# Chunk attention, Fourier mix and MLP on one core: a rest tile mixed in one piece, four transform parts open at once, last stores on two queues

## The chip, the cores and the metric

The kernel runs on 1 core of one Trainium2 chip. Its time is the device time of one execution in microseconds (us), as the median of several runs. A profile is a record of one execution on the same hardware; its span runs from the first to the last instruction of the core.

## The reference

The inputs are `q`, `k`, `v` of shape (8, 8, 576, 64), that is 8 sequences, 8 heads, 576 tokens and 64 features a head, and two MLP weights. Attention is within chunks of 64 tokens; the heads are then put side by side, so that `x` has 8 sequences of 576 tokens with 512 features, and this follows:

```python
X = np.fft.fft(x, axis=1)          # over the 576 tokens
X = np.fft.fft(X, axis=2)          # over the 512 features
mixed = np.real(X).astype(np.float32)
u = x + mixed
mu = np.mean(u, axis=-1, keepdims=True)
var = np.mean((u - mu) ** 2, axis=-1, keepdims=True)
un = (u - mu) / np.sqrt(var + 1e-06)
ch = np.maximum(un @ w_ch1, 0.0) @ w_ch2     # 512 -> 2048 -> 512
return (u + ch).astype(np.float32)
```

All of it is in float32.

## The kernel before, in words

**Tiles and groups.** The tokens lie in tiles of 128 rows. A sequence has 9 chunks of 64 tokens: two LO tiles (chunks from the front), two HI tiles (chunks from the back, held mirrored), and its middle chunk, which shares a "rest" tile (kind `RE`) with the middle chunk of the next sequence. There are 8 groups of four tiles, one for each sequence, and a ninth group, the last, of the four rest tiles. The MLP runs over the groups in turn: `up_first`, `up_plain` and `down_plain` for the first ones, `up_halves` and `down_halves` for the others, where each matrix product is done as seven products of half matrices (lines 1017 and 1064) and weights are fetched from DRAM again for each group.

**Who does what in between.** While the MLP of one group keeps TensorE busy, the attention and the Fourier mix of the next sequence `b` are made in a side generator (`side`, attention and then `fourier(b)`). The loop at the end of the kernel takes one step of the MLP, then so many steps of the side generator as are due. The order of instructions on each engine is this written order; no scheduler changes it. So a step of `fourier` on TensorE stands between two steps of the MLP, and what ScalarE must copy for it has the length of an MLP step to be done.

**The Fourier mix.** Symmetry folds the tokens and features first (`fold`): for each sequence there are two tiles `pm` with 128 token rows, and `pm_rest` for the middle chunk, with 64 token rows for each of its entries. `pm_rest` holds parts 0 and 2 on rows 0 to 63 and parts 1 and 3 on rows 64 to 127. Then:

- The token transform makes four parts T = 0 to 3 (even and odd features, cosine and sine). `product` (line 647) multiplies the fold with the table `tk`: for each part two products over 128 rows with 289 columns, and one over 64 rows with 289 columns. The 64-row products use one half of the array's rows, and those of even and of odd T use different halves. For part 2 there are 12 more, each with a single output row of about 73 columns (`mids`), on four column parts of the array; they write into free columns of part 2's PSUM bank.
- Each part is held in one PSUM bank. The kernel before opens two banks (`z`, from the pool `ps_t` of two), makes parts 0 and 1, lets ScalarE copy them out, takes one step of the MLP, and then makes parts 2 and 3 with `mids` in the same two banks.
- ScalarE copies each part into `zf` (256 columns, line 672) and `zr` (33 and 31 columns, lines 673 and 675: the middle chunk's tokens). `zr` has a half `h` for each of the two sequences that share a rest tile.
- The feature transform `mixed(i)` (line 699) multiplies the columns of `zf`, 128 at a time, with the four tables `ce`, `co`, `cx`, `so`. This gives one 128 by 512 tile in PSUM. For an odd sequence it starts with the rest tile (`i == NM`), made before in two halves of 64 rows with four products each.
- `y`, `both` and `added` add the result to `x`, `means` takes the statistics, and `normed` and `turned` make the MLP's input of it.

The first sequence has a function of its own, `fourier_early`, which opens all four parts at once already (lines 744 and 747), before the MLP starts.

**The end.** The last group's tiles are rest tiles. `store` writes each as two chunks, and each chunk as 63 rows and one row, all issued by SyncE (lines 864 and 865). The last tiles are ready when the last of TensorE's products has been added by VectorE (line 1084).

Of the kernel before, what the change touches and what calls it, by code (L numbers as in the profile page):

```python
# [8 lines left out]
FP32 = mybir.dt.float32  # L9
U32 = mybir.dt.uint32  # L10
ACTF = mybir.ActivationFunctionType
# [5 lines left out]
def kernel(  # L17
# [32 lines left out]
    nc = tc.nc  # L50
    B, H, S, D = q.shape
    DM = H * D
    DFF = w_ch1.shape[1]
    CH = 64
    NC = S // CH
    NM = 2
# [5 lines left out]
    HM, HQ = DM // 2, DM // 4  # L62
    NQ = S // 2 + 1
    NS = (NQ + 3) // 4
    NL = 128 * NM
# [3 lines left out]
    scale = 1.0 / float(D) ** 0.5  # L69

    const = ctx.enter_context(tc.tile_pool(name="const", bufs=1))
# [4 lines left out]
    ps_t = ctx.enter_context(tc.tile_pool(name="ps_t", bufs=2, space=bass.MemoryType.PSUM))  # L76
    ps_a = ctx.enter_context(tc.tile_pool(name="ps_a", bufs=1, space=bass.MemoryType.PSUM))
# [8 lines left out]
    ce = const.tile([128, HQ + 1], FP32, name="ce")  # L86
    co = const.tile([128, HQ], FP32, name="co")
    cx = const.tile([128, HM], FP32, name="cx")
    so = const.tile([128, HQ], FP32, name="so")
# [36 lines left out]
    groups = [[at[what, b, i] for i in range(NM) for what in (LO, HI)] for b in range(B)]  # L126
# [35 lines left out]
    start = one_p.tile([128, KF * 512], FP32, tag="big", name="start")  # L162
# [459 lines left out]
        yield ready(hi)  # L622


    zr = const.tile([128, 2, 4, CH], FP32, name="zr")

    def means(ns):
        st = sm_p.tile([128, 2, 2], FP32, tag="st", bufs=6 + NP, name="st")
# [10 lines left out]
    def fourier(b):  # L639
        h = b % 2  # L640
        zf = one_p.tile([128, 4 * NL + 64], FP32, tag="zf", name="zf")
        zf = zf[:, 0:4 * NL].rearrange("p (t f) -> p t f", t=4)
        pm = [pms.pop((b, i)) for i in range(NM + 1)]

        def product(T, i, out_, lhsT, start, stop, cols=slice(0, NQ)):
            p = slice(0, 128) if i < NM else slice(T % 2 * CH, T % 2 * CH + CH)
            nc.tensor.matmul(
                out=out_, lhsT=lhsT[p], rhs=tk[p, i, T // 2 if T != 5 else 0, cols],
                start=start, stop=stop, skip_group_check=True,
            )  # L650

        for pair in range(2):
            z = [ps_t.tile([128, 512], FP32, tag="pt", name="z") for _ in range(2)]
            for k in range(2):
                T = 2 * pair + k
                for i in range(NM):
                    product(T, i, z[k][:, 0:NQ], pm[i][:, T * HQ:(T + 1) * HQ], i == 0, False)
            for k in range(2):
                product(2 * pair + k, NM, z[k][:, 0:NQ], pm[NM][:, pair * HQ:(pair + 1) * HQ], False, True)
            mids = []  # L660
            if pair == 1:

                for g, c0 in enumerate(range(0, NQ, NS)):
                    c1 = min(c0 + NS, NQ)
                    mids.append((c0, c1, z[0][32 * g:32 * g + 1, NQ:NQ + c1 - c0]))
                for i in range(NM + 1):
                    for c0, c1, out_ in mids:
                        one = pm[i][:, DM:DM + 1] if i < NM else pm[i][:, 2 * HQ:2 * HQ + 1]
                        product(5, i, out_, one, i == 0, i == NM, slice(c0, c1))
            for k in range(2):  # L670
                T = 2 * pair + k
                nc.scalar.copy(zf[:, T, :], z[k][:, 0:NL])
                nc.scalar.copy(zr[:, h, T, 0:NQ - NL], z[k][:, NL:NQ])
                upper, mirrored = zr[:, h, T, NQ - NL:CH], z[k][:, NQ - 2:NL:-1]
                nc.scalar.activation(out=upper, in_=mirrored, func=ACTF.Copy, scale=-1.0 if pair else 1.0)
                for c0, c1, from_ in mids if k == 0 else ():
                    n = max(0, min(c1, NL) - c0)
                    if n > 0:
                        nc.scalar.copy(zf[0:1, T, c0:c0 + n], from_[:, 0:n])
                    if c1 > NL:  # L680
                        nc.scalar.copy(zr[0:1, h, T, 0:NQ - NL], from_[:, n:])
                        nc.scalar.copy(zr[0:1, h, T, NQ - NL:CH], from_[:, NQ - 2 - c0:NL - c0:-1])
            yield

        def mixed(i):
            mix = ps_t.tile([128, 512], FP32, tag="pt", name="mix")
            if i == NM:
                parts = [(j * CH, CH, zr[:, j]) for j in range(2)]
            else:
                parts = [(0, 128, zf[:, :, 128 * i:128 * (i + 1)])]  # L690
            for p0, np_, zt in parts:
                o = mix[p0:p0 + np_]
                for T, (cols, tab) in enumerate((
                    (slice(0, HM + 1, 2), ce),
                    (slice(1, HM, 2), co),
                    (slice(0, DM, 2), cx),
                    (slice(HM + 1, DM, 2), so),
                )):
                    nc.tensor.matmul(
                        out=o[:, cols], lhsT=zt[:, T], rhs=tab,  # L700
                        start=(T == 0), stop=(T == 3), skip_group_check=True,
                    )
            y = three_p.tile([128, XW], FP32, tag="y", name="y")
            nc.scalar.copy(y[:, 0:HM + 1], mix[:, 0:HM + 1])
            nc.scalar.copy(y[:, DM:DM + 1], mix[:, 0:1])
            return y, mix

        def both(y, mix):
            nc.vector.tensor_tensor(out=y[:, DM - 1:HM:-1], in0=y[:, 1:HM], in1=mix[:, HM + 1:DM], op=ALU.subtract)
            nc.vector.tensor_tensor(out=y[:, 1:HM], in0=y[:, 1:HM], in1=mix[:, HM + 1:DM], op=ALU.add)  # L710
            return y

        def added(y, n):
            x, w = xt(n), DM + (kind(n) == HI)
            eng = nc.gpsimd if kind(n) == HI else nc.vector
            eng.tensor_tensor(out=x[:, 0:w], in0=y[:, 0:w], in1=x[:, 0:w], op=ALU.add)  # L716

        for i in ((NM,) if h == 1 else ()) + tuple(range(NM)):
            y = both(*mixed(i))
            ns = [rests[b // 2]] if i == NM else [at[LO, b, i], at[HI, b, i]]  # L720
            for n in ns:
                added(y, n)
            means(ns)
            yield

    def fourier_early():
# [3 lines left out]
        zf = one_p.tile([128, 4 * NL + 64], FP32, tag="zf", name="zf")  # L730
        zf = zf[:, 0:4 * NL].rearrange("p (t f) -> p t f", t=4)
        pm = [pms.pop((0, i)) for i in range(NM + 1)]
        z = [ps_t.tile([128, 512], FP32, tag="pt", name="z") for _ in range(2)]
        more = ps_a.tile([128, 2, 512], FP32, tag="att", name="more_z")
        z += [more[:, k] for k in range(2)]
        mid = ps_f.tile([128, 512], FP32, tag="ff", name="mid")
        mids = [(c0, min(c0 + NS, NQ)) for c0 in range(0, NQ, NS)]
        order = (1, 0, NM)
        for i in order:
            at_ = {"start": i == order[0], "stop": i == order[-1], "skip_group_check": True}  # L740
            for T in range(4):
                p = slice(0, 128) if i < NM else slice(T % 2 * CH, T % 2 * CH + CH)
                d0_ = T * HQ if i < NM else T // 2 * HQ
                nc.tensor.matmul(out=z[T][:, 0:NQ], lhsT=pm[i][p, d0_:d0_ + HQ], rhs=tk[p, i, T // 2], **at_)
            p, d0_ = (slice(0, 128), DM) if i < NM else (slice(CH, 128), 2 * HQ)
            for r, (c0, c1) in enumerate(mids):
                nc.tensor.matmul(
                    out=mid[32 * r:32 * r + 1, 0:c1 - c0], lhsT=pm[i][p, d0_:d0_ + 1], rhs=tk[p, i, 0, c0:c1], **at_
# [8 lines left out]
        for r, (c0, c1) in enumerate(mids):  # L757
            n, from_ = min(c1, NL) - c0, mid[32 * r:32 * r + 1]
# [2 lines left out]
            else:  # L761
                nc.scalar.copy(zf[0:1, 2, c0:c0 + n], from_[:, 0:n])
        for T in range(4):
            nc.scalar.copy(zr[:, 0, T, 0:NQ - NL], z[T][:, NL:NQ])
            upper, mirrored = zr[:, 0, T, NQ - NL:CH], z[T][:, NQ - 2:NL:-1]
            nc.scalar.activation(out=upper, in_=mirrored, func=ACTF.Copy, scale=1.0 if T < 2 else -1.0)
            if T == 2:
                n = NL - c0
                nc.scalar.copy(zr[0:1, 0, T, 0:NQ - NL], from_[:, n:c1 - c0])
                nc.scalar.copy(zr[0:1, 0, T, NQ - NL:CH], from_[:, NQ - 2 - c0:n:-1])  # L770
        yield
        for i in range(NM):
            for T, tab in ((0, cos_d), (1, cos_d), (3, sin_d), (2, sin_d)):
                nc.tensor.matmul(
                    out=early_xp[0][i][:, T % 2::2], lhsT=zf[:, T, 128 * i:128 * (i + 1)], rhs=tab[:, T % 2::2],
# [78 lines left out]
    def store(n, o):  # L854

        if kind(n) == LO:
            b, c = chunks(n)[0]
            to = out[b, c * CH + 1:c * CH + 129, :].rearrange("(c p) d -> c p d", c=2)
            nc.sync.dma_start(out=to[:, ::-1], in_=o)
            return  # L860
        for h, (b, c) in enumerate(chunks(n)):
            r0, t0 = h * CH, c * CH
            if kind(n) == RE:
                nc.sync.dma_start(out=out[b, t0 + 1:t0 + CH, :], in_=o[r0 + 1:r0 + CH])
                nc.sync.dma_start(out=out[b, 0:1, :], in_=o[r0:r0 + 1])
            else:
                nc.sync.dma_start(out=out[b, t0:t0 + CH, :], in_=o[r0:r0 + CH])

# [248 lines left out]
    with tc.manual_schedule():  # L1117
# [73 lines left out]
        t = 0  # L1191
# [84 lines left out]
```

## Time and profile before

| what | value |
|---|---|
| time, median of 3 runs | 1115.54 us (1113.27 to 1116.66) |
| span of the profiled execution | 1113.4 us |
| TensorE products (PE) busy | 1085.2 us, 97% |
| VectorE (DVE) busy | 582.7 us, 52% |
| ScalarE (ACT) busy | 297.7 us, 27% |
| GpSimd (POOL) busy | 277.7 us, 25% |
| granted clock of TensorE | 1.0 |
| `z` products of line 647, 128 rows x 289 columns | 112 records, mean 407 ns |
| rest's `mix` products of line 699, 64 columns of the array | 64 records |

A float32 product leaves two records in the trace, so counts there are twice those in the program. The duration of a record is its latency; records overlap, and what a product costs TensorE is read from the distance between starts. In lines of the timeline the columns are the start and the length in us, the engine, the line of the kernel, the operation, output and inputs, shapes, the number of records, and in brackets idle time before it with what ended it. "SPq" is SyncE's queue of DMA issues.

### The profile page before, as it was taken

What the parts mean: (1) busy time and instruction counts of PE and PEld (TensorE: products, weight loads), DVE (VectorE), ACT (ScalarE), POOL (GpSimd) and SP (SyncE); (2) the same over time, 40 slices, a digit from 0 to 9 for tenths busy, and PEclk for the clock granted to TensorE, in tenths of its full rate; (3) what the DMA queues carried; (4) which work ended last, traced back from release to release, by engine and by line L of the source; (5) the groups of instructions that cost most, each with busy time, mean ns of one, the idle gap of its engine ahead of it and who ended that gap; (6) DMA issues with size and microseconds to landing.
All of it is one profiled execution on the core that took longest, in us unless ns stands there. A gap on an engine that the chain in (4) does not pass through costs nothing. (4 is left out here: it accounts for less than half of the span.)

```text
span 1113.4 us, 18823 instructions
## 1 busy us (share of the span) xinstructions
PE 1085.2 (97%) x7042; PEld 848.6 (76%) x7042; DVE 582.7 (52%) x1260; ACT 297.7 (27%) x725; POOL 277.7 (25%) x403
## 2 busy tenths in 40 slices
PE   8899999999999999999999999999999999999998
PEld 6644454447887888888888888788888888888887
DVE  4799987324556365653555355625554434323521
ACT  4688553222112311322022212221133102201210
POOL 4200102454305140244024220424042401120130
PEclk9999999999999999999999999999999999999999
DMA  8766556689567546682558356763653355446232
GB/s 164 229 184 193 159 157 225 186 244 296 175 176 201 155 138 197 200 244 107 171 167 236 121 170 206 195 188 130 198 171 109 114 167 189 137 152 198 86 114 76
DMA packets 147970, 192.73 MB, mean 173 GB/s; under 512 B 66126, under 2 KB 104014, under 8 KB 140712
## 3 DMA queue, kind: packets, MB, share of 16 engines
q1 hardware_dynamic: 145768, 190.46, 56.3%
q8 instruction: 56, 0.92, 0.3%
q0 software_dynamic: 512, 0.68, 0.3%
q10 hardware_dynamic: 1600, 0.39, 0.2%
q14 instruction: 34, 0.28, 0.1%
HBM read 167.22 MB, written 24.12 MB: 172 GB/s over the span
## 5 line engine op out<-in xcount | busy, mean ns | idle before, releaser
L923 POOL TENSOR_TENSOR h<-h 128x256 f32<-128x256 f32 x64 | 55.8, 878 | 272.6 <-PE pb L1017 153.1
L1064 PE MATMUL pa<-wb,h 128*128 128x256 f32 x512 | 114.8, 381 | 0.0
L1064 PE MATMUL pb<-wb,h 128*128 128x256 f32 x512 | 114.2, 380 | 0.0
L1017 PE MATMUL pb<-unT,wa 128*128 128x256 f32 x448 | 107.0, 382 | 4.1 <-DVE wa L1026 3.7
L1017 PE MATMUL pb<-wa 128*128 128x256 f32 x448 | 107.5, 383 | 2.5 <-DVE h L1034 2.5
L1064 PEld LDWEIGHTS pa<-wb,h 128*128 128x128 f32 x512 | 96.2, 190 | 14.2 <-issue 1.6
L1017 PE MATMUL pa<-unT,wa 128*128 128x256 f32 x448 | 106.6, 381 | 0.0
L1064 PEld LDWEIGHTS pb<-wb,h 128*128 128x128 f32 x512 | 96.1, 190 | 12.5
L1017 PEld LDWEIGHTS pb<-unT,wa 128*128 128x128 f32 x448 | 84.1, 190 | 19.3 <-DVE wa L1026 8.3
L1017 PEld LDWEIGHTS pb<-wa 128*128 128x128 f32 x448 | 83.6, 190 | 16.1 <-DVE h L1034 3.7
L1017 PEld LDWEIGHTS pa<-unT,wa 128*128 128x128 f32 x448 | 84.0, 190 | 11.1
L933 PE MATMUL up<-unT,wa 128*128 128x512 f32 x128 | 58.0, 600 | 2.0 <-ACT h L941 1.2
L971 PE MATMUL dn<-wb,h 128*128 128x512 f32 x128 | 57.6, 598 | 1.3 <-ACT h L941 1.3
L1064 PE MATMUL pa<-wb,yall 128*128 128x256 f32 x256 | 58.2, 382 | 0.0
L1064 PE MATMUL pb<-wb,yall 128*128 128x256 f32 x256 | 57.1, 381 | 0.0
L950 PE MATMUL up<-unT,wa 128*128 128x512 f32 x128 | 56.8, 596 | 0.0
L1064 PE MATMUL pb<-wb 128*128 128x256 f32 x256 | 56.6, 379 | 0.0
L1032 ACT ACTIVATE h<-pa 128x256 f32<-128x256 f32 x56 | 21.5, 383 | 131.3 <-PE pa L1017 131.3
L1024 DVE TENSOR_TENSOR wa<-pa,wa 128x256 f32<-128x256 f32 x56 | 23.8, 425 | 61.4 <-PE pa L1017 60.0
L1017 PE MATMUL pa<-wa 128*128 128x256 f32 x224 | 53.2, 381 | 0.7 <-ACT wa L1022 0.7
L1064 PEld LDWEIGHTS pb<-wb,yall 128*128 128x128 f32 x256 | 48.2, 190 | 6.5
L1064 PEld LDWEIGHTS pb<-wb 128*128 128x128 f32 x256 | 48.3, 190 | 6.2
(235 smaller groups left out, 1664.9 us busy)
## 6 DMA issues: line engine op xcount, KB each, us to landing
wb<-s SPq DMA_DIRECT2D x56, 1024.0 KB
wa<-s SPq DMA_DIRECT2D x196, 256.0 KB
xall<-in_moe_w_ch_dram SPq DMA_DIRECT2D x22, 512.0 KB
q<-in_q_dram SPq DMA_DIRECT2D x96, 112.0 KB
k<-in_k_dram SPq DMA_DIRECT2D x96, 112.0 KB
v<-in_v_dram SPq DMA_DIRECT2D x124, 64.0 KB
yall<-in_moe_w_ch_dram SPq DMA_DIRECT2D x10, 512.0 KB
s<-wb SPq DMA_DIRECT2D x20, 256.0 KB
```

What stands on the lines that cost most here:

```text
L923: nc.gpsimd.tensor_tensor(out=h1[:, m, hi], in0=h1[:, m, lo], in1=h1[:, m, hi], op=ALU.subtract)
L933: nc.tensor.matmul(out=up, lhsT=w1[:, kk, m * 128:(m + 1) * 128], rhs=unT[:, kk], start=(kk == 0), stop=(kk == KD - 1),)
L950: nc.tensor.matmul(out=up, lhsT=w1[:, kk, m * 128:(m + 1) * 128], rhs=unT[:, kk], start=(kk == 0), stop=(kk == KD - 1),)
L971: nc.tensor.matmul(out=dn, lhsT=h1[:, m, s * 128:(s + 1) * 128], rhs=w2[:, m, :], start=(m == 0), stop=(m == KF - 1),)
L1017: nc.tensor.matmul(out=dst, lhsT=w[:, kk, r], rhs=rhs[o][:, kk], start=(o in (0, 2) and kk == 0), stop=(kk == 1), skip_group_check=True,)
L1024: nc.vector.tensor_tensor(out=b, in0=dst, in1=a, op=ALU.add)
L1032: nc.scalar.activation(out=h1[:, m, lo], in_=dst, func=ACTF.Relu)
L1064: nc.tensor.matmul(out=dst, lhsT=lhs[:, m], rhs=w[:, m], start=(o in (0, 2) and m == 0), stop=(m == HF - 1), skip_group_check=True,)
```

## The change

There are three parts. First, `zr` is laid out with the two sequences' halves side by side in each part, so the rest tile is mixed as 128 rows in four products, where there were eight with 64 rows. Second, all four parts of the token transform are open at once: parts 2 and 3 get the two PSUM banks of the attention's scores (`ps_a`, tag "att"). The first step makes the 128-row products of parts 0 and 1, the second step those of parts 2 and 3, then the 64-row products of all four parts one after the other, then `mids`, and then ScalarE copies all four parts out. So all products on parts of the array stand together. Third, for the second and the fourth tile of the last group, the second chunk's stores are issued by ScalarE and not by SyncE.

```diff
-    zr = const.tile([128, 2, 4, CH], FP32, name="zr")
+    zr = const.tile([128, 4, 2, CH], FP32, name="zr")
...
-        for pair in range(2):
-            z = [ps_t.tile([128, 512], FP32, tag="pt", name="z") for _ in range(2)]
-            for k in range(2):
-                T = 2 * pair + k
-                for i in range(NM):
-                    product(T, i, z[k][:, 0:NQ], pm[i][:, T * HQ:(T + 1) * HQ], i == 0, False)
-            for k in range(2):
-                product(2 * pair + k, NM, z[k][:, 0:NQ], pm[NM][:, pair * HQ:(pair + 1) * HQ], False, True)
...
+        z = [ps_t.tile([128, 512], FP32, tag="pt", name="z") for _ in range(2)]
+        more = ps_a.tile([128, 2, 512], FP32, tag="att", name="more_z")
+        z += [more[:, k] for k in range(2)]
+        for T in range(4):
+            for i in range(NM):
+                product(T, i, z[T][:, 0:NQ], pm[i][:, T * HQ:(T + 1) * HQ], i == 0, False)
+            if T == 1:
+                yield
+        for T in range(4):
+            product(T, NM, z[T][:, 0:NQ], pm[NM][:, T // 2 * HQ:(T // 2 + 1) * HQ], False, True)
...
+        for T in range(4):
+            nc.scalar.copy(zf[:, T, :], z[T][:, 0:NL])
+            nc.scalar.copy(zr[:, T, h, 0:NQ - NL], z[T][:, NL:NQ])
...
-            if i == NM:
-                parts = [(j * CH, CH, zr[:, j]) for j in range(2)]
-            else:
-                parts = [(0, 128, zf[:, :, 128 * i:128 * (i + 1)])]
-            for p0, np_, zt in parts:
-                o = mix[p0:p0 + np_]
...
+            zt = zr.rearrange("p t h f -> p t (h f)") if i == NM else zf[:, :, 128 * i:128 * (i + 1)]
+            for T, (cols, tab) in enumerate((
...
             if kind(n) == RE:
-                nc.sync.dma_start(out=out[b, t0 + 1:t0 + CH, :], in_=o[r0 + 1:r0 + CH])
-                nc.sync.dma_start(out=out[b, 0:1, :], in_=o[r0:r0 + 1])
+                eng = nc.scalar if n in groups[-1][1::2] and h else nc.sync
+                eng.dma_start(out=out[b, t0 + 1:t0 + CH, :], in_=o[r0 + 1:r0 + CH])
+                eng.dma_start(out=out[b, 0:1, :], in_=o[r0:r0 + 1])
```

`fourier_early` changes only in the indices of `zr`.

## The prediction

> **What bounds the kernel now.** I read the totals first, then the chain that ended last, then TensorE's timeline around one token transform, the rest tile's mix, ScalarE's timeline beside them, the waits, and the last microseconds.
>
> ```profile
> PE 1085.2 (97%) x7042; PEld 848.6 (76%) x7042; DVE 582.7 (52%) x1260; ACT 297.7 (27%) x725; POOL 277.7 (25%) x403
> ...
> 1094.92 13.83 PE pb L1064 x64
> ...
> 1108.84 0.42 DVE wb L1084
> ...
> 260.39 2.11 PE L647 MATMUL z<-tk,pm 128*128 128x289 f32 x8
> 262.43 0.76 PE L647 MATMUL z<-tk,pm_rest 64*128 64x289 f32 x4
> 263.12 3.72 PE L1064 MATMUL pa<-wb,h 128*128 128x256 f32 x16
> 266.68 2.11 PE L647 MATMUL z<-tk,pm 128*128 128x289 f32 x8
> 268.72 0.76 PE L647 MATMUL z<-tk,pm_rest 64*128 64x289 f32 x4
> 269.40 0.43 PE L647 MATMUL z<-tk,pm 128*1 128x73 f32 x16
> ...
> 270.00 3.72 PE L1064 MATMUL pa<-wb,yall 128*128 128x256 f32 x16
> 273.56 0.39 PE L699 MATMUL mix<-ce,zf 128*128 128x129 f32 x2
> ```
>
> TensorE is busy for 97% of the span, no other engine for more than 52%, and the chain from 884 us to the end is TensorE alone, followed by one addition and the last stores. So time taken from TensorE's order comes off the end, one for one. The waits view supports it: TensorE waits some 23 us in all, in pieces of at most 2.4 us, and none of the waits after the first 20 us is for a DMA.
>
> The eight lines are sequence 2's transform. A stretch costs what lies between its start and the next one's: first step 260.39 to 263.12, 2.73 us, second step 266.68 to 270.00, 3.32 us.
>
> ```profile
> 36.82 1.14 PE L744 MATMUL z<-tk,pm 128*128 128x289 f32 x4
> 37.79 1.14 PE L744 MATMUL more_z<-tk,pm 128*128 128x289 f32 x4
> ...
> 39.10 0.76 PE L744 MATMUL z<-tk,pm_rest 64*128 64x289 f32 x4
> 39.69 0.66 PE L744 MATMUL more_z<-tk,pm_rest 64*128 64x289 f32 x4
> 40.27 0.31 PE L747 MATMUL mid<-tk,pm_rest 64*1 64x73 f32 x8
> ```
>
> This is the first sequence's transform, which has its four 64-row products in a row already: 39.10 to 40.27, 1.17 us for 8 records. Two such products, 4 records, cost 0.68 us above (262.43 to 263.12, 268.72 to 269.40). Four 128-row records in full mode take 37.79 - 36.82 = 0.97 us, so eight take 1.94.
>
> ```profile
> 388.08 0.43 PE L699 MATMUL mix<-ce,zr 128*64 128x129 f32 x2
> ...
> 389.81 3.72 PE L1064 MATMUL pa<-wb,yall 128*128 128x256 f32 x16
> 393.37 0.39 PE L699 MATMUL mix<-ce,zf 128*128 128x129 f32 x2
> ...
> 394.47 0.81 PE L1064 MATMUL pa<-wb,yall 128*128 128x256 f32 x3
> ```
>
> The rest tile's mix in two halves holds TensorE for 1.73 us, the mix of a full tile with the same four tables for 1.10 us.
>
> ```profile
> 151.54 2.22 PE L647 MATMUL z<-tk,pm 128*128 128x289 f32 x8 [0.81 <-ACT zr L675]
> ...
> 271.94 0.22 ACT L675 ACTIVATE zr<-z 128x31 f32<-128x31 f32 x1
> ...
> 1109.29 0.28 SPq L864 DMA_DIRECT2D out_dram<-wb  x1
> ...
> 1110.23 0.28 SPq L865 DMA_DIRECT2D out_dram<-wb  x1
> ```
>
> The first line is the one transform where TensorE waits for ScalarE to free the two banks (sequence 1). The second is the last of ScalarE's copies after sequence 2's second step: it ends at 272.16, and the mix that needs it starts at 273.56. The last two are SyncE's first and last issue of the four stores that follow the last addition.
>
> **What the Trainium skill says.** "TensorEngine Tiling (Array Packing)", Tiling Modes, says that a change of tiling mode drains TensorE. The trace agrees, and gives the price. Entry: four `more_z` records are followed after 1.07 us and not 0.97 (37.79 to 38.86), 0.09 to 0.10. Return: 16 MLP records after a mix of 64 columns take 393.37 - 389.81 = 3.56 us, and in full mode 3.46 (274.65 to 278.11), 0.10. "TensorE: Matmul & The Clock Gate", Part 3, says that products on different row groups run at once, and that weights load beside a running product only when the row group differs or a background buffer is free. The trace agrees for the halves by rows: two products take 0.68 us, which is two passes of 0.24 and a load and a drain of 0.10 each. For the halves by columns it agrees only in part: 1.73 us is far over half of what the same products would take one after the other. "DMA: Bandwidth & Descriptors", Issuing engines are not separate DMA queues, says that a second issuing engine saves only the time to issue. Here that is 0.3 us a store.
>
> **The change part by part.**
>
> First step of the transform. It loses the 64-row products of parts 0 and 1, with both changes of mode. Before: 2.73 us and 0.10 for the return in the MLP step behind it, 2.83. After: eight full-mode records, 1.94. It saves 0.89.
>
> Second step. It gets those two products, in the stretch that is on half the array anyway. By the first sequence's lines four of them take 1.17 us, so 1.17 - 0.68 = 0.49 more. The 12 `mids`, the drain and the return stay. The net of both steps is 0.89 - 0.49 = 0.40 us. Seven sequences use this code (1 to 7): **2.8 us**. All of it is TensorE's own time between MLP steps, so it is on the path. If parts 2 and 3 did not run behind parts 0 and 1 without a new drain, they would cost 0.68, the net would be 0.21, and seven make 1.5. I take 0.40, since the very order was measured.
>
> Rest's mix. Before: the entry of 0.09, then 1.73, then the return of 0.10, that is 1.92 us. After: as a full tile, 1.10, with no change of mode. It saves 0.82 us. Sequences 1, 3, 5 and 7 do it: **3.3 us**. The new layout of `zr` puts the 128 weights of a part side by side as in `zf`; ScalarE's copies keep their count and shapes.
>
> The wait of sequence 1. The step before it starts at 147.03 and its 8 records take 3.53 us elsewhere (160.33 to 163.86), so the second step was due at 150.56 and starts at 151.54; that step is then 3.43 us and not 3.32. With banks of its own, part 2 need not wait for ScalarE: 0.98 + 0.11 = 1.09 us at most. But ScalarE is still in the last weight conversions then (152.55 to 154.54), and all copies are now behind them. TensorE would reach the rest's mix at about 157.0 (144.30 + 1.94 + 3.43 + 3.81 + 3.53); copies that start at 154.5 and take 2.9 us end at 157.4. The four products of the mix wait for their parts one by one, so that 0 to 0.5 us comes back. I take **0.9 us**.
>
> ScalarE's burst. Copies of all four parts now stand in one step. In order of its queue: parts 0 and 1 take 0.87 us (263.22 to 264.1), parts 2 and 3 with the small rows 2.0 (270.14 to 272.16). ScalarE takes instructions strictly in order, so what stands behind the burst is the MLP's copy `wa<-pa`, the copy `y` and the statistics, and the mix waits for the burst. For even sequences one MLP step of 3.56 us lies in between. Parts 0 and 1 don't wait for `mids`: in the first sequence the first copy starts at 39.88, 0.78 us after the 64-row products began. So they are done while TensorE runs the rest of the step, and the end of the burst stays where it is, 1.4 us ahead of the mix. Even if they began only at the step's end, 2.9 us would fit in 3.56. For odd sequences after the first, 6.9 us lie in between. Cost: 0.
>
> Banks. `more_z` takes the bank pair of the scores. The attention of the same sequence has ended by then, and the next one's scores start after the last mix, at least two MLP steps of 3.5 us behind the copies. `z` stays open over one MLP step, in which nothing is turned (the MLP's input of the next group is turned after the mix). Cost: 0.
>
> Last stores. SyncE issues four stores in a row, at 1109.29, 1109.61, 1109.91 and 1110.23; data move from 1110.0 to 1112.0 and the span ends at 1113.4. With two of them on ScalarE, idle by then, the last issue starts at about 1109.61, 0.62 us earlier. The same DMA engines carry both chunks, so the data may take longer once they overlap: 0 to 0.6, and I take **0.5 us**. The other tile's stores are 3 us before the end and cost nothing.
>
> The sum is 2.8 + 3.3 + 0.9 + 0.5 = 7.5 us, and 1115.5 - 7.5 = 1108.0 us.
>
> **The rivals.**
>
> *The halves don't run on.* Parts 2 and 3 pay a load and a drain of their own (1.5 and not 2.8), and overlapping stores bring nothing: 1.5 + 3.3 + 0.9 = 5.7, 1109.8 us. Against it: the first sequence's lines.
>
> *ScalarE's burst becomes the wait.* The copies begin late, behind relu or conversions, and the mix waits some 0.7 us in each of seven sequences: 7.5 - 4.9 = 2.6, 1112.9 us. For it: the slack at even sequences is only 1.4 us and sequence 1 has seen such a wait. Against it: ScalarE is idle 2.9 us before each such group of copies at even sequences, and 27% busy in all.
>
> *The gain is given back elsewhere.* TensorE comes sooner to points that VectorE sets (its waits for VectorE at line 1017 add up to 6.2 us) and half is lost: 1111.8 us. Against it: these stand between products of the same step, and VectorE's work there follows from TensorE's own results.
>
> *Slower.* The scores' banks are not free at the second step, or the next scores wait for copies, by 1.5 us for each sequence: 10.5 - 7.5 = 3 us more than before, 1118.5 us. Against it: the order of the changed build has whole MLP steps on both sides.
>
> **How the numbers follow.** My forecast has 0.68; halves that don't run on 0.10; given back elsewhere 0.09; the burst as a wait 0.09; slower 0.04. The bound for faster by 0.3% is 1112.2 us. The forecast and the first rival lie below it, and so does most of the one given back; the burst lies in the band of no change. That makes 0.87 faster, 0.09 same, 0.04 slower. Single runs of before differ by 3.4 us, so a median may be off by 1 us either way. The range goes down to 1105.0 (all bounds at their best give 7.8 us less, 1107.7, and runs may lie 2.7 below) and up to 1111.8, which takes in the first rival and half of what is given back.
>
> **What would show it right or wrong.** In the trace after: a first step of 1.94 us with no 64-row products in it; a second of 3.8 us with eight 64-row records in about 1.17; the rest's mix in 1.10 us with no gap on either side; no wait of line 647 for ScalarE near 150 us, and no new wait of the mix; last issues of SyncE and ScalarE side by side. The prediction is wrong if the mix waits for `zr` or `zf`, if the four 64-row products take 1.4 us, or if TensorE's waits for VectorE grow by as much as the steps shrink.

## The result, and the profile after

The changed kernel takes 1108.9 us, the median of 6 runs (1107.21 to 1110.2). The kernel before, run beside it, takes 1115.12 us (6 runs). The ratio is 0.9946, 95% interval 0.9933 to 0.9958. So 6.2 us went, where 7.5 were forecast. The totals on the page of the kernel after hardly differ from those of before, but for TensorE's:

```profile
PE 1079.4 (97%) x7010; PEld 849.1 (77%) x7010; DVE 582.1 (53%) x1260; ACT 297.5 (27%) x725; POOL 277.4 (25%) x403
```

TensorE's busy time fell by 5.8 us (1085.2 to 1079.4), at the same share of a shorter span. TensorE's timeline of the kernel after, at sequence 2's transform, shows where (start and length in us, line, operation, shapes, records):

```profile
260.04 2.11 PE L647 MATMUL z<-tk,pm 128*128 128x289 f32 x8
261.99 3.62 PE L1061 MATMUL pa<-wb,h 128*128 128x256 f32 x16
265.44 2.11 PE L647 MATMUL more_z<-tk,pm 128*128 128x289 f32 x8
267.48 0.76 PE L647 MATMUL z<-tk,pm_rest 64*128 64x289 f32 x4
268.07 0.66 PE L647 MATMUL more_z<-tk,pm_rest 64*128 64x289 f32 x4
268.66 0.43 PE L647 MATMUL more_z<-tk,pm 128*1 128x73 f32 x16
...
269.25 3.72 PE L1061 MATMUL pa<-wb,yall 128*128 128x256 f32 x16
272.81 0.39 PE L695 MATMUL mix<-ce,zf 128*128 128x129 f32 x2
```

The first step lasts from 260.04 to 261.99, 1.95 us, and holds no product on part of the array. The second lasts from 265.44 to 269.25, 3.81 us; its eight 64-row records take 268.66 - 267.48 = 1.18 us. The MLP step between the two takes 3.45 us (261.99 to 265.44), with no return from another mode in it, where the one behind the second step takes 3.56 (269.25 to 272.81). The steps have the lengths that the prediction named, to 0.01 us.

ScalarE's timeline of the kernel after, for the same transform, first and last copy:

```profile
268.27 0.37 ACT L673 COPY zf<-z 128x256 f32<-128x256 f32 x1 [2.26 <-PE z L647]
...
271.20 0.22 ACT L676 ACTIVATE zr<-more_z 128x31 f32<-128x31 f32 x1
```

The copies begin 0.79 us after the 64-row products do, and don't wait for `mids`; they end at 271.42, 1.39 us ahead of the mix. The burst costs nothing here.

The rest tile's mix of sequence 3, TensorE's timeline of the kernel after:

```profile
386.85 0.39 PE L695 MATMUL mix<-ce,zr 128*128 128x129 f32 x2
...
387.95 3.62 PE L1061 MATMUL pa<-wb,yall 128*128 128x256 f32 x16
```

It holds TensorE for 1.10 us where it was 1.73, and the MLP step behind it is a full-mode step. Sequence 1, where the kernel before waited for ScalarE, in TensorE's timeline of the kernel after:

```profile
146.74 3.59 PE L968 MATMUL dn<-wb,h 128*128 128x512 f32 x8
150.17 2.11 PE L647 MATMUL more_z<-tk,pm 128*128 128x289 f32 x8
...
153.98 3.70 PE L968 MATMUL dn<-wb,h 128*128 128x512 f32 x8
157.52 0.39 PE L695 MATMUL mix<-ce,zr 128*128 128x129 f32 x2
```

The wait is gone, and none took its place at the mix: it starts 3.54 us after the start of the MLP step ahead of it, the length of such a step (3.53). ScalarE's copies ran from 155.06 to 157.94, so the last ended after the mix had begun; each product waits for its own part only, and the fourth began at 158.40.

Two things did not go as forecast. The first is a wait of TensorE for the scores of sequence 2. From the timelines of the kernel after, the issues of SyncE (SPq), the transpose on VectorE that needs the load of `k`, and the scores:

```profile
220.40 1.48 SPq L881 DMA_DIRECT2D s<-wb  x3
221.93 0.80 SPq L881 DMA_DIRECT2D s<-wa  x1
222.83 1.05 SPq L881 DMA_DIRECT2D s<-wb  x1
223.92 0.72 SPq L881 DMA_DIRECT2D s<-wa  x1
224.74 2.34 SPq L194 DMA_DIRECT2D k<-in_k_dram  x4
...
229.43 1.08 DVE L348 STREAM_TRANSPOSE kT<-k 128x512 f32<-128x512 f32 x1 [6.43 <-DMA k<-in_k_dram]
...
230.56 0.69 PE L380 MATMUL sc<-kT,qT 64*64 64x64 f32 x32 [1.65 <-DVE rd L441]
```

And the same in the kernel before, from the same three timelines:

```profile
225.02 2.37 SPq L194 DMA_DIRECT2D k<-in_k_dram  x4
...
229.74 1.12 DVE L348 STREAM_TRANSPOSE kT<-k 128x512 f32<-128x512 f32 x1 [6.08 <-DMA k<-in_k_dram]
...
230.91 0.69 PE L380 MATMUL sc<-kT,qT 64*64 64x64 f32 x32 [0.19 <-DVE kT L348]
```

The releaser is named `rd` in one and `kT` in the other, but `rd` is a 0.17 us operation behind the same transpose, which itself had been waiting 6.43 us for `k`. The four loads of `k` stand in SyncE's order behind a set of stores, those of the converted weights (`s<-wa`, `s<-wb`, written out for later groups). Counted from the MLP's first product (54.01 after, 53.51 before), `k` was issued at 170.7 us after and at 171.5 before, only 0.8 us earlier, while TensorE had gained 2.3 us in sequence 1. The difference, 1.5 us, is the growth of the wait from 0.19 to 1.65.

The second is the end. The last lines of the whole timeline of the kernel after:

```profile
1103.48 0.42 DVE L1081 TENSOR_TENSOR wb<-pb,wb 128x256 f32<-128x256 f32 x1 [3.10 <-PE pb L1061]
1103.93 0.28 SPq L861 DMA_DIRECT2D out_dram<-wb  x1
1103.94 0.29 ACTq L861 DMA_DIRECT2D out_dram<-wb  x1
1104.25 0.26 SPq L862 DMA_DIRECT2D out_dram<-wb  x1
1104.26 0.36 ACTq L862 DMA_DIRECT2D out_dram<-wb  x1
```

The last issue starts 0.78 us after the last addition's start and no longer 1.39 us. Yet from the end of that addition to the end of the span it is 1108.17 - 1103.91 = 4.3 us, against 1113.42 - 1109.26 = 4.2 before. Windows of half a microsecond of the kernel after; the last three numbers are the granted clock, the mean busy share of the 16 DMA engines and GB/s:

```profile
1104.50:1105.00 0.50, 0.00 (x0) 0.00 (x0) 0.00 (x0) 0.00 (x0) 0.00 (x0) 1.00 0.46 115
1105.00:1105.50 0.50, 0.00 (x0) 0.00 (x0) 0.00 (x0) 0.00 (x0) 0.00 (x0) 1.00 0.51 102
1105.50:1106.00 0.50, 0.00 (x0) 0.00 (x0) 0.00 (x0) 0.00 (x0) 0.00 (x0) 1.00 0.50 164
1106.00:1106.50 0.50, 0.00 (x0) 0.00 (x0) 0.00 (x0) 0.00 (x0) 0.00 (x0) 1.00 0.38 143
```

By the packets of the trace, SyncE's queue moves data from 1104.69 to 1106.47, 0.76 us after its issue, and ScalarE's queue only from 1105.68 to 1106.59, 1.74 us after its own. Together they take 1.90 us, where SyncE's queue alone took 1.94 in the kernel before (1110.04 to 1111.98). So issuing together did not make the data move together, and SyncE's queue, with half the bytes it had before, took 1.78 us for them. The engines are about half busy on average meanwhile (0.38 to 0.51).

### The profile page after: what moved, and what is told of

Same layout as the page of the kernel before. It is cut to its first block, busy times and chain, and to the rows that moved or that the text cites. A ratio compares the mean times of both kernels' runs of the same rounds, so it can differ in the third digit from the quotient of the medians.

```text
span 1108.2 us, 18749 instructions
## 1 busy us (share of the span) xinstructions
PE 1079.4 (97%) x7010; PEld 849.1 (77%) x7010; DVE 582.1 (53%) x1260; ACT 297.5 (27%) x725; POOL 277.4 (25%) x403
```

## The experiments

To see single terms I cut the span at fixed points of TensorE's order. T1 is sequence 1 from the first product of its transform to its last mix product; "even" (sequences 2, 4, 6) and "odd" (3, 5, 7) are the same for the others. G2 and G4 are the stretches in front of sequences 2 and 4, from the last mix of the sequence before: MLP steps and attention. "Body" runs from the MLP's first product to the end of the last addition, "tail" from there to the end of the span. The MLP's first product itself lies anywhere from 51.7 to 55.6 us in these profiles, in kernels that do the same up to there; "body" leaves that out. All in us, one profile each.

| kernel | T1 | even | odd | G2 | G4 | body | tail |
|---|---|---|---|---|---|---|---|
| before | 21.65 | 18.71 | 25.81 | 94.44 | 100.48 | 1055.8 | 4.2 |
| e3_stores_only | 21.56 | 18.71 | 25.82 | 95.17 | 100.42 | 1056.2 | 4.2 |
| e12_before_paced | 21.73 | 18.71 | 25.81 | 94.02 | 100.32 | 1054.2 | 4.2 |
| e1_mix_only | 20.91 | 18.71 | 24.99 | 95.06 | 101.99 | 1053.9 | 4.2 |
| e2_parts_only | 20.17 | 18.31 | 25.42 | 94.96 | 100.37 | 1051.6 | 4.2 |
| after | 19.35 | 18.31 | 24.59 | 95.90 | 100.49 | 1049.9 | 4.3 |
| e4_no_act_stores | 19.35 | 18.31 | 24.59 | 95.66 | 101.08 | 1050.0 | 4.2 |
| e5_both_on_act | 19.36 | 18.31 | 24.59 | 95.50 | 101.11 | 1050.2 | 4.2 |
| e10_early_half | 19.35 | 18.31 | 24.59 | 95.18 | 101.10 | 1049.7 | 3.4 |
| e9_conv_paced | 19.35 | 18.31 | 24.59 | 94.34 | 101.15 | 1049.4 | 4.2 |
| e11_paced_early_half | 19.35 | 18.31 | 24.59 | 94.02 | 100.99 | 1048.9 | 3.4 |

**The parts of the change, one at a time.** The rest's mix alone (the layout of `zr` and the four products, all else as before):

```diff
-            if i == NM:
-                parts = [(j * CH, CH, zr[:, j]) for j in range(2)]
...
+            zt = zr.rearrange("p t h f -> p t (h f)") if i == NM else zf[:, :, 128 * i:128 * (i + 1)]
```

> The kernel before with the rest tile mixed as 128 rows alone. Theory (gains ahead of sequence 2's late k load are lost, all others count): four times 0.83 us of TensorE time, but sequence 1's share is mostly lost in a longer wait of the scores (line 380) at about 230 us, which grows from 0.19 us to 0.7 to 1.0; 2.5 to 2.9 us less than before. Rival (every gain counts): 3.3 us less, the wait at 230 us as before.

Measured: 1112.87 us, ratio 0.9966 (0.9957 to 0.9975), 3.8 us of 1116.82. Odd sequences lose 0.82 us, even ones nothing. The rival's 3.3 us lies nearer than the theory's 2.5 to 2.9, but the interval, 2.8 to 4.8 us, parts them only in part. The wait for the scores is 0.81 us, in the theory's range; e3_stores_only, below, has 0.92 with the old transform, so this is no proof of growth. The four parts open at once alone, with the mix in two halves:

```diff
...
+        more = ps_a.tile([128, 2, 512], FP32, tag="att", name="more_z")
+        z += [more[:, k] for k in range(2)]
...
```

> The kernel before with the four parts open at once alone. Theory: seven times 0.40 us and 1.09 us for sequence 1's wait, of which sequence 1's 1.5 us is mostly lost at about 230 us, where the scores' wait grows from 0.19 us to about 1.3; 2.5 to 2.9 us less than before. Rival (every gain counts): 3.9 us less, the wait at 230 us as before. The rest tile's mix keeps its 1.73 us.

Measured: 1111.02 us, ratio 0.9959 (0.9944 to 0.9973). Even sequences lose 0.40 us, odd ones 0.39, and sequence 1 loses 1.48, that is 0.40 and 1.08 for its wait. The theory, 2.5 to 2.9 us, fell: the ratio gives 4.6 us (3.0 to 6.3), which takes in the rival's 3.9, and the wait for the scores is 0.71 us and not 1.3. By their ratios the two parts add up to 8.4 us, with 1.9 us either way, and the whole change to 6.2, with 0.7; that is just compatible. By the bodies in the table they add up to 6.5 (2.1 and 4.4), and the whole gives 6.0. The stores alone:

```diff
+                eng = nc.scalar if n in groups[-1][1::2] and h else nc.sync
+                eng.dma_start(out=out[b, t0 + 1:t0 + CH, :], in_=o[r0 + 1:r0 + CH])
...
```

> The kernel before with ScalarE's stores alone. Theory: the stores of ScalarE's queue start to move data some 1.7 us after their issue and not 0.75, so the time from the last addition's end to the span's end stays at 4.1 to 4.3 us and the time is the same within 0.3 us. Rival (the prediction's step): 3.6 us there, and 0.5 us less than before.

Measured: 1115.72 us, ratio 0.9998 (0.9986 to 1.0011); the tail is 4.2 us. By the packets ScalarE's data again start 1.70 us after their issue. And the changed kernel without them:

```diff
-                eng = nc.scalar if n in groups[-1][1::2] and h else nc.sync
-                eng.dma_start(out=out[b, t0 + 1:t0 + CH, :], in_=o[r0 + 1:r0 + CH])
...
+                nc.sync.dma_start(out=out[b, t0 + 1:t0 + CH, :], in_=o[r0 + 1:r0 + CH])
...
```

> The changed kernel with all stores on SyncE again. Theory: as the changed kernel within 0.3 us, 4.1 to 4.2 us from the last addition's end to the span's end. Rival (ScalarE's stores cost what the forecast missed): 0.5 to 1 us faster than the changed kernel. The wait at 230 us is 1.4 to 1.7 us in both.

Measured: 1109.29 us, ratio 0.9942 (0.9925 to 0.9958); the tail is 4.2 us. The stores on ScalarE are worth nothing from either side. The times alone would not show half a microsecond, since the intervals reach 1.4 us and more to each side; the tails do, at 4.2 us for one issuer and 4.2 to 4.3 for two.

This run and e3_stores_only also show how the wait for the scores scatters. Up to the last stores e3_stores_only has the code of the kernel before, and its wait is 0.92 us and not 0.19. So the pair before/after overstates the growth. Mean G2 of the two profiles of the old transform is 94.80 us. The four profiles with the whole new transform and the old order of issue (after, e4_no_act_stores, e5_both_on_act, e10_early_half) have 95.56, so about 0.8 us is given back there. The single profiles scatter by 0.7 us. With e7_seq1_old, below, whose sequence 1 is old too, the old mean is 94.92, and it is 0.6 us.

**Why the second queue brings nothing.** Either ScalarE's queue starts slowly by itself, or the two queues hold each other up. Both stores of a last tile on ScalarE, none on SyncE:

```diff
-                eng = nc.scalar if n in groups[-1][1::2] and h else nc.sync
+                eng = nc.scalar if n in groups[-1][1::2] else nc.sync
```

> The changed kernel with both chunks of the second and fourth tile of the last group stored by ScalarE, none of their stores on SyncE. Theory[...]: with nothing of SyncE beside them ScalarE's first store moves data 0.7 to 0.8 us after its issue, and the end is 4.1 to 4.3 us after the last addition. Rival (ScalarE's queue is slower in itself): 1.7 us, and an end at 5 us or more.

Measured: 1110.51 us in a single run, beside 1116.19 for the kernel before; the tail is 4.2 us. By the packets of the trace, ScalarE's queue alone moves data 0.76 us after its issue (1104.61 to 1105.37), as SyncE's does alone (1109.29 to 1110.04 in the kernel before); beside SyncE's it took 1.74. The slowness belongs to the pair, and not to ScalarE's queue. What the two share, no run shows.

**Does sequence 1's gain count at all?** It lies ahead of the wait for the scores. The changed kernel with all stores on SyncE, and with the old transform and the old rest's mix in sequence 1 alone:

```diff
+        if b == 1:
+            for pair in range(2):
+                z = [ps_t.tile([128, 512], FP32, tag="pt", name="z") for _ in range(2)]
...
+        else:
             z = [ps_t.tile([128, 512], FP32, tag="pt", name="z") for _ in range(2)]
...
```

> The changed kernel, all last stores on SyncE, with sequence 1 alone in the old form (two parts at a time, rest tile in two halves). Theory: TensorE has 2.3 us more to do near 150 us, but the scores' wait at about 230 us shrinks from 1.4 us to under 0.5, so that the time from the MLP's first product to those scores grows by some 0.9 us only; 5 to 5.7 us less than before. Rival (every gain counts): 2.3 us slower than the changed kernel, 4 us less than before, the wait unchanged.

Measured: 1112.5 us, ratio 0.9967 (0.9955 to 0.9978), so 3.7 us below the kernel before. My theory, that the wait swallows most of sequence 1's gain, fell: most of the gain counts. In the profile T1 is 21.73 us, the wait for the scores 0.90 and G2 95.16, so of 2.4 us in T1 some 0.4 come back in G2. (One other wait, 2.23 us in sequence 5's stretch, is this profile's own.)

**Taking the stores out of `k`'s way.** First with the stores of the converted weights issued by GpSimd, the changed kernel with all last stores on SyncE otherwise:

```diff
-            nc.sync.dma_start(out=to[:, :, o, kk], in_=a.rearrange("p (a x) -> p a x", a=2))
+            nc.gpsimd.dma_start(out=to[:, :, o, kk], in_=a.rearrange("p (a x) -> p a x", a=2))
```

> The changed kernel, all last stores on SyncE, and the stores of the first weights' half matrices (the helper keep1, near 190 to 240 us) issued by GpSimd and not by SyncE, so that the loads of k no longer stand behind them. Theory: sequence 2's k lands before TensorE needs it, the scores' wait near 230 us (1.4 to 1.7 us) falls under 0.3, and the kernel is 1.3 to 2 us faster than the changed one, 7.5 to 8.5 less than before. Rival (the late load is bound by the transfers themselves, or the wait only moves): the wait stays over 1 us or comes back within the next 100 us, and the time is as the changed kernel's.

Measured: 1126.83 us, ratio 1.0103 (1.0087 to 1.0118), slower than the kernel before. SyncE's issues and TensorE's timeline in this run:

```profile
208.16 6.35 SPq L194 DMA_DIRECT2D k<-in_k_dram  x4
214.61 8.19 SPq L217 DMA_DIRECT2D v<-in_v_dram  x4
...
227.69 1.13 PE L380 MATMUL sc<-kT,qT 64*64 64x64 f32 x32 [14.51 <-DVE rd L441]
...
244.69 0.65 PE L380 MATMUL sc<-kT,qT 64*64 64x64 f32 x32
```

The scores that the theory was about are the last line, one round of the attention later than those of 227.69, and they no longer wait. But the round ahead of them, which in e4_no_act_stores starts at 213.48 us without a wait, now waits 14.51 us. Its `k` is issued from 208.16 us and transposed at 226.56, 18.4 us later, where in e4_no_act_stores it was 8.8 (203.46 to 212.29). SyncE's order had also held the stores back: a store could not start before the loads ahead of it were issued. On GpSimd they go out as soon as their data are ready, and the 16 DMA engines are 0.89 to 0.99 busy from 208 to 220 us. The four loads of `v` above are all issued at 222.8 us, where in e4_no_act_stores it was 216.7, though seven stores stood ahead of them there. That the stores compete with the loads fits all of this, and no run shows it alone. While TensorE stood still its granted clock fell to 0.50; the 24 records of the MLP behind the wait took 11.45 us, against 10.40 for those in e4_no_act_stores. So the diagnosis stands, and the remedy opened a larger wait. The same with an addition for the tail, the right halves of the last tiles stored a step early (the diff is shown with e10_early_half below):

> As the kernel with the stores of keep1 on GpSimd, and in the last group the right half of each second-half tile's columns, final one product earlier, is stored then, so that only 1 KB a row is left after the last addition. Theory: the time from the last addition's end to the span's end falls from 4.15 us to 3.4 to 3.8, the rest as in that kernel; 8 to 9 us less than before. Rival (the tail is fixed latency, not data): 4.1 us still.

Measured: 1123.85 us, ratio 1.007 (1.0052 to 1.0088), a wait of 16.17 us at the round where e6_conv_stores_pool had 14.51, and a tail of 3.6 us, where that kernel's was 4.5.

Then by order alone. All stores stay on SyncE, and the conversion is stepped a little slower at first, so that its stores are issued behind the load of `k`:

```diff
-                    for _ in range(3):
+                    for _ in range(2 if t < begin[1] + 4 else 3):
                         next(conv1, None)
```

> The changed kernel with all stores on SyncE, and with the conversion of the kept weights stepped 2 instead of 3 per MLP step in the first four steps of sequence 2's stretch, so that its stores stand behind the load of k in SyncE's order. Theory (scores wait for the transpose of a k that was issued behind those stores): the wait of TensorE near 230 us falls from about 1.4 us to under 0.5, the stretch from sequence 1's last mix to sequence 2's first z to 94.3 to 94.9 us from 95.5 to 95.9, and the time lies 0.8 to 1.3 us below that kernel's with 3 steps: some 1108. Rival (that stretch is set by how many bytes the DMA engines can move, whatever the order of issue): the wait moves to another load or to the down weights, the stretch stays at 95.5 to 95.9 or grows, and the time is the same or longer.

Measured: 1109.0 us, ratio 0.9931 (0.9911 to 0.9951); the kernel before, run beside it, gave 1115.27. SyncE's issues, VectorE's transpose and TensorE's scores in this run's timelines:

```profile
217.10 2.38 SPq L194 DMA_DIRECT2D q<-in_q_dram  x4
219.58 2.66 SPq L194 DMA_DIRECT2D k<-in_k_dram  x4
222.29 0.43 SPq L880 DMA_DIRECT2D s<-wa  x1
...
224.57 1.12 DVE L348 STREAM_TRANSPOSE kT<-k 128x512 f32<-128x512 f32 x1 [0.41 <-DMA k<-in_k_dram]
...
229.29 0.65 PE L380 MATMUL sc<-kT,qT 64*64 64x64 f32 x32
```

`k` now goes ahead of the stores and its transpose is done 3.6 us before the scores, which start without a wait. From issue to transpose it is 5.0 us here and 4.7 in the kernel after, so what decided was when `k` was issued. G2 fell to 94.34 us, as the theory had it. The 0.8 to 1.3 us did not show in the time: the medians of this kernel and of e4_no_act_stores, taken at different times, are 0.3 us apart and the intervals of their ratios overlap widely. The body is only 0.6 us shorter, as the stretch in front of sequence 5 took 0.7 us more in this profile.

**The tail.** In the last group the right 256 columns of each last tile are final one step before the left ones. With all stores on SyncE they are stored then:

```diff
+                    if g == NG - 1:
+                        store(high, ohigh, slice(HM, DM))
...
-                    store(high, ohigh)
+                    store(high, ohigh, slice(0, HM if g == NG - 1 else DM))
```

> The changed kernel with all stores on SyncE, and with the right 256 columns of the last tiles stored as soon as they are final, one step ahead, so that only the left half goes out after the last addition. Theory (what follows the last addition is issue, a fixed wait and the bytes of the last stores): the time from the last addition's end to the end of the span falls from 4.15 to 4.2 us to 3.5 to 3.8, and the time by about 0.5 us. Rival (that time is a fixed latency that doesn't know of bytes): 4.1 us or more, and no difference.

Measured: 1108.6 us, ratio 0.9926 (0.9907 to 0.9946). The end of the timeline in this run:

```profile
1103.29 0.42 DVE L1082 TENSOR_TENSOR wb<-pb,wb 128x256 f32<-128x256 f32 x1 [3.10 <-PE pb L1060]
1103.74 0.28 SPq L860 DMA_DIRECT2D out_dram<-wb  x1
...
1104.69 0.26 SPq L861 DMA_DIRECT2D out_dram<-wb  x1
```

SyncE issues the same four stores over the same 1.2 us, with half the bytes, and the span ends at 1107.1, 3.4 us after the addition. By the packets the data move from 1104.50 to 1105.66, in 1.16 us where the full bytes take 1.94, and these 0.78 us are what the tail lost (4.2 to 3.4 us). So the tail depends on the bytes that are left. Bringing the last issue forward by 0.6 us, in the change itself, gave nothing. The expected 0.5 us of the time can't be told: the interval overlaps that of e4_no_act_stores.

**Both edits.**

> Both edits together. If both theories hold, 1.3 to 1.8 us below the changed kernel with all stores on SyncE, 7.5 to 8.5 us below the kernel before, ratio about 0.993. If only the early halves work, ratio about 0.994; if neither, the ratio of the changed kernel, 0.9946, or above.

Measured: 1107.3 us (1104.23 to 1108.92), ratio 0.9913 (0.9889 to 0.9937), the lowest of the study and well below the kernel before. Against the changed kernel the interval of the ratio just overlaps (0.9933 to 0.9958), so the times alone don't prove it faster. Its profile shows the two pieces: G2 is 94.02 us, the tail 3.4, and the span 1106.4 against 1108.2 with the MLP's first product at the same place (54.09 and 54.01).

**The same pacing in the kernel before.** If the queue of stores were the only way in which the gain comes back, both kernels paced would lie the whole 7 us apart:

> The kernel before with the same pacing of the weights' conversion, 2 instead of 3 steps in the first four MLP steps of sequence 2's stretch. Theory (without the queue of stores ahead of k, the scores wait in neither kernel, and the change's gain before sequence 2 is kept whole): the wait near 230 us, 0.19 and 0.92 in the two profiles of the old transform, is gone, the stretch from sequence 1's last mix to sequence 2's first z is 94.0 to 94.4 us as in the changed kernel with this pacing, from the MLP's first product to the last addition 1055.1 to 1056 us, so 6.5 to 7.2 us above the changed kernel with this pacing (1049.4), and the time is 0 to 0.8 us below the kernel before. Rival (the shorter wait in the kernel before is the transfers' own pace and not the order of issue): the stretch stays at 94.4 to 95.2 us and the two kernels with this pacing lie 6 us apart or less.

Measured: 1115.47 us against 1115.48, ratio 0.9996 (0.9987 to 1.0005). The wait is gone and G2 is 94.02 us, as expected. The distance is not settled. By the medians the two paced kernels lie 6.5 us apart (1115.47 and 1109.0), by the ratios 0.65% or 7 us, with 2.4 us either way. By the bodies of the two profiles they lie only 4.8 us apart, less than the theory allows. In that profile the kernel before, paced, spends 0.8, 0.6 and 0.7 us less than e9_conv_paced in front of sequences 4, 5 and 6; it has no wait at all at a place in front of sequence 6 where the two other profiles of the old transform wait 1.2 us. The waits that I followed are of one kind: in VectorE's order a transpose of `q`, which waits for its load, stands ahead of an addition of the MLP that TensorE needs. In e4_no_act_stores, VectorE and then TensorE:

```profile
472.79 1.11 DVE L348 STREAM_TRANSPOSE qT<-q 128x512 f32<-128x512 f32 x1 [0.61 <-DMA q<-in_q_dram]
473.74 0.73 DVE L1022 TENSOR_TENSOR wa<-pb,wa 128x256 f32<-128x256 f32 x2
...
474.20 1.13 PE L1013 MATMUL pb<-unT,wa 128*128 128x256 f32 x4 [0.82 <-DVE wa L1022]
```

In the kernel after, VectorE's transpose did not wait here and TensorE waited 0.21 us; in e9_conv_paced TensorE waited 1.12. In front of sequence 4 all profiles of the whole new transform but one show some 0.6 us more than those of the old (column G4); in front of sequence 6 they show 0.2 us less on average than the two profiles of the old order of issue. One profile for each kernel can't tell a part of the gain given back from the scatter of such waits, and this stays open.

## Why the prediction was right, and where not

The direction, the size and the mechanism were right: the time lies 0.9 us above the forecast. The terms, as the table has them:

- **Transform, 0.40 us for each of seven sequences.** Right: 18.71 to 18.31 us in even sequences, and 0.39 to 0.40 in odd ones by e2_parts_only alone. Both halves of it were read from the kernel before itself, one from the first sequence, which had the new order already. The rival that the halves don't run on is refuted by the 1.18 us of eight records. Beyond four passes of 0.24 us some 0.2 us are left there, the same as in the 0.68 of four records; that this is a load and a drain of 0.10 each, as the prediction has it, no run shows. "TensorE: Matmul & The Clock Gate", Part 3, says that products on different row groups run at once, and this trace agrees: those eight records take 1.18 us, where eight in full mode take 1.95.
- **Rest's mix, 0.82 us in four sequences.** Right: 25.81 to 24.99 us by e1_mix_only alone.
- **Sequence 1's wait, 0.9 us.** The bound given with it, 1.09, was the right value: 1.08 by e2_parts_only. The part taken off for a wait of the mix did not come, since the mix starts on the first part while ScalarE still copies the fourth.
- **ScalarE's burst and the banks, 0.** Right: 1.39 us of room in front of sequence 2's mix, where 1.4 was read from before, and no wait for a bank of the scores behind a copy.
- **Last stores, 0.5 us.** This step failed. It took the last issue as what the end follows, and allowed only for data that overlap. The tail is 4.2 us before and 4.3 after, and 4.2 in e3_stores_only. What it depends on is the bytes, by e10_early_half. "DMA: Bandwidth & Descriptors", Issuing engines are not separate DMA queues, says that a second issuer saves only the time to issue; here not even that came off the end.
- **What the sum left out.** It took each microsecond off TensorE's order to come off the end, and named as support that no wait after the first 20 us is for a DMA. That reading was too narrow: the waits view names the last releaser, and VectorE's transpose hides the load behind it. In front of sequence 2 some 0.8 us are given back, and e9_conv_paced shows by what: the wait goes when `k` is issued ahead of the stores. This is the rival "given back elsewhere" in small, at another place than it named: not at the MLP's additions for themselves, but at loads that SyncE issues in their turn.

The sum by the table is 2.30 for sequence 1, 3 x 0.40 and 3 x 1.22, that is 7.16 us, against 7.0 forecast for these three terms. Less 0.76 in front of sequence 2 and nothing for the stores, it leaves 6.4; 6.2 was measured. So the forecast owes little to luck: of its misses only the 0.2 us of sequence 1's wait goes the other way. The bodies give nearly the same: 1056.0 us on average for the old transform (two profiles), 1050.0 for the new (four), 6.0 apart. The 0.2 to 0.4 that remain are within the scatter of the small waits.

## What to carry to other kernels

Read the price of products on part of TensorE's array from a place of the same trace that already has the order you want: here that gave 0.40 us for each transform and 0.82 for each rest's mix, and both came true. When a tuned kernel's bound engine is to gain in the middle, look ahead of the gain for the next point that is paced by something else, and read it two steps back: from the waiting product to the operation that releases it, and from that to the load it waits for and to what stands ahead of that load in its issuing queue. Moving queued stores to another issuer may undo an order that protected the loads; reorder them within the queue first. At the end of a kernel, leave fewer bytes behind the last result, and measure before you count on issuing them from two engines: here that gave nothing.

## What the hardware showed that was not expected

- Two queues issued within 0.01 us of each other did not start together: SyncE's data came after 0.76 us, ScalarE's after 1.74 (1.70 in e3_stores_only), while ScalarE's alone came after 0.76.
- With stores issued by GpSimd beside them, SyncE's issues of loads took longer: four of `k` and four of `v` took 14.6 us to issue (208.16 to 222.80; 15.0 in e8_conv_pool_early_half), against 6.1 for the same eight in e4_no_act_stores, seven stores between them left out.
- The start of the MLP, before which these kernels do the same work, lies anywhere from 51.7 to 55.6 us, so a comparison of single spans to better than a few us needs a mark behind it.
